# The last batch's second step in one go, its inverse blocks moved behind the first count

## The chip, the cores and the metric

The kernel runs on one core of a Trainium2 chip. The metric is device time in microseconds (us), the median of the runs of a kernel. A profiled run also leaves a trace, whose own time and span stand in the table below. On this core PE (TensorE) does matmuls and transposes, DVE (VectorE), ACT (ScalarE) and POOL (GpSimd) do the elementwise work, and SP (SyncE), ACT and POOL issue DMAs.

## The reference

The input `x` has 8 batches of 2496 tokens with 256 columns. Each batch is filtered along its tokens in the frequency domain; then 19968 tokens go to 8 experts.

```python
X = np.fft.rfft(x, axis=1)
Y = X * (filt_r + 1j * filt_i)[None]
x = np.fft.irfft(Y, n=2496, axis=1).reshape(19968, 256)
logits = x @ w_gate                       # 19968 x 8
order = np.argsort(-logits.flatten())     # greedy, best pair first
for idx in order:
    tok, e = idx // 8, idx % 8
    if assigned[tok] >= 0 or counts[e] >= 2496:
        continue
    assigned[tok] = e; counts[e] += 1
for e in range(8):
    out[assigned == e] = np.maximum(x[assigned == e] @ w1[e], 0) @ w2[e]
```

## The kernel before, in words

**The filter.** 2496 is split into 39 by 64, so each transform has two steps of small matmuls. Per batch, `s1` is the first forward step. `s2` is the second: four matmuls with `cW` (L241), two DVE products with the filter (L247 into `P`, L248 into `Q`), and a POOL subtraction and addition (L249, L250), after which `P` holds a block of the spectrum. There are ten such blocks in a batch, and `Q` has one buffer. `tr` turns blocks with four transposes on PE into PSUM (L260, tile `pa`). `split` casts the turned block on ACT to `yh` (L281), and takes the rest `yl` as the turned block minus `yh` (L282), so that a matmul works with two rounded parts. `inv1` is the first inverse step of one of ten blocks `q`: for each of two halves three matmuls (L296: `cEh` by `yh`, `cEh` by `yl`, `cEl` by `yh`), a copy to `zt` (L308) and two DMAs to a buffer `zd` in DRAM (L310).

**The gate on the side.** The logits are linear in the spectrum. The gate is multiplied into the blocks of the spectrum (L269), the result is turned (`trv`, L288), and `v1` (L328), a transpose (L344), `v2` (L354) and `v3` (`lg`, L356) run the same two inverse steps on the 8 columns of the logits. The routing can begin when the logits of all batches are there, before the tokens themselves.

**The second inverse step.** It is cut into 40 units (a batch and a fifth of its columns). A unit is loaded from `zd` (`load_z`, L377), multiplied by `cD` in three parts (two of 512 columns, one of 256: L403), each part is copied to `xo` (L404), and the unit is stored to `xs` in DRAM (L407). Units of the first two batches run in the transform; the other 30, `rest`, run beside the routing. While the transform's buffers still stand, stores go from two `xo` tiles or from parts of an old `Y1` tile; a new pool takes their place in front of unit 15.

**The routing.** `threshold` searches each expert's threshold in 11 rounds. A round builds the comparison `Gm` on DVE (L564, two pieces), counts with 11 matmuls (L572), takes `t`, `D` and `X` from the count on DVE (L580 to L582), spreads it over all partitions with one matmul (L585, called the broadcast product here), and takes the next threshold from it on DVE (L609, L622, L624, L602, L605). The rounds are a chain PE, DVE, PE, DVE. Then places and lists are made (L712 to L772), tokens are gathered from `xs` with indirect DMAs on POOL (L825), turned (L839) and put through the experts' two matmuls (L861, L904) to the end of the kernel.

**What sets the order.** `run` puts the transform's steps into a list of events with a slot number (ten slots a batch) and a priority, and emits them in order of slot. A scheduler then places each engine's instructions by its own estimate of the timeline, except where `manual_schedule` asks for an engine's order of emission; before, that holds for PE from the first broadcast product on. Beside the rounds, `Pump` takes pieces from the generator `after()`, which yields an estimated cost for each part of a unit and for each of the five `inv1` of the last batch that are left to it. Of the last batch, `q` from 5 are copied by ACT to a buffer `y7` when they are turned (`y7b`), and `split` by ACT and POOL when their `inv1` comes.

Of the kernel before, what the change touches and what calls it, by code (L numbers as in the profile page):

```python
# [15 lines left out]
G = 22  # L16
# [116 lines left out]
class Fft:  # L133


    def __init__(s, tc, i, xs, zd, lg, pp):
        s.tc, s.nc, s.i, s.xs, s.zd, s.lg, s.pp = tc, tc.nc, i, xs, zd, lg, pp
        s.zw = s.zo = s.y7 = s.y9 = None
# [97 lines left out]
    def s2(s, b, g, dh):  # L236

        nc = s.nc
        p = s.ps.tile([128, 4, 128], F32, name="p2", tag="b", bufs=2)
        for k in range(4):  # L240
            nc.tensor.matmul(p[:, k], s.Y1[b][:, 4*g+k, dh*128:dh*128+128], s.cW[:, 4*g+k], start=True, stop=True)  # L241
        P = s.yt[b, g, dh] = s.wp.tile([128, 4, 128], F32, name="P", bufs=NP)
# [9 lines left out]
    def tr(s, b, q):  # L252

        nc = s.nc
        g, k = q // 2, 2 * (q % 2)
        yt = [s.yt[b, g, dh] for dh in range(2)]
        p = s.ps.tile([128, 2, D], F32, name="pa", tag="c", bufs=4)
        for h in range(2):
            for dh in range(2):
                nc.tensor.transpose(p[:, h, 128*dh:128*dh+128], yt[dh][:, k+h], s.id)  # L260
        if b == B - 1 and q > 4:
            nc.scalar.copy(s.y7b(q), p)
        else:
            s.split(b, q, p, nc.vector)
        if k:
            p = s.ps.tile([128, 128], F32, name="pv", tag="c", bufs=4)
            for dh in range(2):
                for k in range(4):
                    nc.tensor.matmul(p[32*k:32*k+32], s.gate[:, dh], yt[dh][:, k], start=dh == 0, stop=dh == 1, skip_group_check=True)  # L269
            s.vs[b, g] = s.wp.tile([128, 128], F32, name="vs", bufs=1)  # L270
            nc.scalar.copy(s.vs[b, g], p)

    def y7b(s, q):
        if q == 9 and s.y9 is None:
            s.y9 = s.wp.tile([128, 4, 128], F32, name="P", bufs=NP).rearrange("p k d -> p (k d)")
        y = s.y7[:, 80+512*q:592+512*q] if q < 9 else s.y9
        return y.rearrange("p (k d) -> p k d", d=D)

# [18 lines left out]

    def inv1(s, b, q):
# [5 lines left out]
        p = s.ps.tile([128, 2, D], F32, name="pa", tag="c", bufs=4)  # L304
# [11 lines left out]
    def v1(s, g, b0, b1):  # L316

        nc = s.nc
        if s.y7 is None:
            s.y7 = s.wp.tile([128, K1 * D], F32, name="Y1", tag="Y1", bufs=2)  # L320
            nc.gpsimd.memset(s.y7[:72, :2640].rearrange("p (a n) -> p a n", n=3*G)[:, :, N2:], 0.0)
        c = 8 * (b1 - b0)
        r = slice(64, 64 + c) if b0 else slice(0, c)
        p = s.pt([128, 4, 128], not b0)
        for k in range(4):
            (h, l), (Eh, El) = ([t[:, 4*g+k] for t in ts] for ts in ((s.Vh, s.Vl), s.cE))
            for m, (v, w) in enumerate(((h, Eh), (h, El), (l, Eh))):
                nc.tensor.matmul(p[:c, k], v[:, 8*b0:8*b1], w, start=m == 0, stop=m == 2)  # L328
        z = s.y7[r, :2640].rearrange("p (r k n) -> p k r n", r=2, k=K1)[:, 4*g:4*g+4, :, :N2]
        nc.scalar.copy(z, p[:c].rearrange("p k (r n) -> p k r n", r=2))  # L330

    def v2(s, b0, b1):
# [3 lines left out]
        s.U = s.zp.tile([120, G, c], F32, name="xo", tag="xo", bufs=2)  # L336
        n = 8 if c > 8 else G
        for g0 in range(0, G, n):
# [8 lines left out]
    def v3(s, b0, b1):  # L347

        nc, c = s.nc, 8 * (b1 - b0)
        n = 8 if c > 8 else G  # L350
        for g0 in range(0, G, n):
            g1 = min(g0 + n, G)
            p = s.pt([128, g1 - g0, c], not b0)
            s.lastv = nc.tensor.matmul(p[:120], s.cD, s.U[:, g0:g1], start=True, stop=True).ins  # L354
            with s.tc.issue_after(s.lastq):
                nc.vector.tensor_copy(s.lg[:, b0:b1, g0:g1], p[:117].rearrange("p g (b e) -> p b g e", e=8))  # L356

    def more_z(s, units):
# [3 lines left out]
        y = s.wp.tile([128, 4, 5, D], F32, name="Y1", tag="Y1", bufs=2)  # L362
        s.xos = [y[:120, k] for k in range(4)]
        zs = [f[:120, k] for k in range(4)] + [w[:120, k] for k in range(2)]
# [45 lines left out]
    def run(s, cp, wp, xp, ps, freed, prep, rest):  # L410
# [13 lines left out]
        for b in range(B):  # L424
# [34 lines left out]
        at(10*B - 0.8, 9, s.more_z, rest[3+NZ:9+NZ])  # L459
        at(10*B + 2.9, 3.61, s.more_z2, rest[9+NZ:3+NZ+MZ])  # L460
        at(10*B + 2.9, 3.6, s.v2, B - 1, B)
        at(10*B + 2.9, 3.62, s.v3, B - 1, B)
        at(10*B + 2.9, 3.64, prep, S - G, S)
        for q in (2, 3, 4):
            at(10*B + 2.9, 3.7 + 0.01 * q, s.inv1, B - 1, q)
        for e in sorted(ev, key=lambda e: e[:3]):
            e[3](*e[4])

# [6 lines left out]
class Route:  # L475
# [75 lines left out]
    def counts(s, nj, thr, made=False):  # L551
# [374 lines left out]
def emit(tc, i, out):  # L926
    nc = tc.nc
    with ExitStack() as st:
# [18 lines left out]
        def freed():  # L947
# [187 lines left out]
```

## Time and profile before

| | us |
|---|---|
| runs of the kernel before | 1430.25, 1433.83, 1435.20; median 1433.83 |
| profiled run, its own time | 1429.82 |
| its span | 1428.0 |
| PE busy | 1380.0 (97%) |
| DVE, ACT, POOL busy | 899.9, 681.3, 487.5 |
| mean granted clock of PE | 0.99 |

The page divides the span into 40 slices of 35.7 us. PE is at 9 tenths or more in all but three: the first, the one from 321 to 357 (8) and the one from 393 to 428 (6), in which the last unit ends and the first gathered tokens arrive, and in which the granted clock is below 9 tenths too:

```profile
PE   8999999998969999999999999999999999999998
PEclk9999999999989999999999999999999999999999
DMA  9676675658881022102212212112111321111100
```

Busy shares are of all time, at whatever clock was granted. "Idle before, releaser" in a row is the engine's idle time ahead of an instruction and what ended it.

### The profile page before, as it was taken

What the parts mean: (1) busy time and instruction counts of PE and PEld (TensorE: products, weight loads), DVE (VectorE), ACT (ScalarE), POOL (GpSimd) and SP (SyncE); (2) the same over time, 40 slices, a digit from 0 to 9 for tenths busy, and PEclk for the clock granted to TensorE, in tenths of its full rate; (3) what the DMA queues carried; (4) which work ended last, traced back from release to release, by engine and by line L of the source; (5) the groups of instructions that cost most, each with busy time, mean ns of one, the idle gap of its engine ahead of it and who ended that gap; (6) DMA issues with size and microseconds to landing.
All of it is one profiled execution on the core that took longest, in us unless ns stands there. A gap on an engine that the chain in (4) does not pass through costs nothing. (4 is left out here: it accounts for less than half of the span.)

```text
span 1428.0 us, 27263 instructions
## 1 busy us (share of the span) xinstructions
PE 1380.0 (97%) x10338; PEld 1210.5 (85%) x10338; DVE 899.9 (63%) x2568; ACT 681.3 (48%) x1658; POOL 487.5 (34%) x538
## 2 busy tenths in 40 slices
PE   8999999998969999999999999999999999999998
PEld 8898898885437898888888888889898899899988
DVE  6677676776547769668667875876867635423231
ACT  7766766644464346226335533533623635423231
POOL 3433433431024126323422632433424333323212
PEclk9999999999989999999999999999999999999999
DMA  9676675658881022102212212112111321111100
GB/s 358 225 223 174 217 217 140 148 130 233 321 314 61 29 82 72 41 23 96 63 36 80 68 43 78 56 43 90 58 34 51 124 71 51 43 45 51 40 19 29
DMA packets 58124, 152.59 MB, mean 107 GB/s; under 512 B 10889, under 2 KB 32137, under 8 KB 54409
## 3 DMA queue, kind: packets, MB, share of 16 engines
q1 hardware_dynamic: 29200, 68.79, 15.9%
q0 software_dynamic: 18416, 60.37, 12.9%
q10 hardware_dynamic: 10377, 21.68, 4.6%
q8 instruction: 82, 1.34, 0.4%
q14 instruction: 49, 0.40, 0.1%
HBM read 87.16 MB, written 63.70 MB: 106 GB/s over the span
## 5 line engine op out<-in xcount | busy, mean ns | idle before, releaser
L904 PE MATMUL py<-w1h,hl 128*128 128x256 f32 x2496 | 485.7, 287 | 1.0 <-DVE hl L872 0.7
L904 PEld LDWEIGHTS py<-w1h,hl 128*128 128x128 f32 x2496 | 403.0, 191 | 7.3 <-issue 3.2
L904 PE MATMUL py<-w1l,hl 128*128 128x256 f32 (+1 forms) x1280 | 359.5, 283 | 0.0
L915 POOL DMA_INDIRECT out<-y,oid x160 | 169.1, 1057 | 506.7 <-ACT y L914 456.5
L867 ACT ACTIVATE hl<-pz 128x512 fp32r<-128x512 f32 (+1 forms) x320 | 187.4, 588 | 226.7 <-PE pz L861 203.1
L861 PE MATMUL pz<-xo,w0h 128*128 128x512 f32 (+1 forms) x640 | 264.3, 413 | 3.0 <-DVE hl L869 1.5
L869 DVE SCALAR_TENSOR_TENSOR hl<-pz,hl 128x512 fp32r<-128x512 f32 x256 | 175.4, 688 | 144.8 <-ACT hl L867 143.4
L861 PE MATMUL pz<-z,w0h 128*128 128x512 f32 (+1 forms) x640 | 248.7, 389 | 0.0
L861 PE MATMUL pz<-xo,w0l 128*128 128x512 f32 (+1 forms) x640 | 248.6, 388 | 0.0
L904 PEld LDWEIGHTS py<-w1l,hl 128*128 128x128 f32 (+1 forms) x1280 | 241.8, 189 | 1.9
L825 POOL DMA_INDIRECT xg<-xs,xid x160 | 170.4, 1065 | 129.8 <-issue 54.2
L914 ACT COPY y<-py 128x256 f32<-128x256 f32 x152 | 56.6, 372 | 305.8 <-PE py L904 262.6
L861 PEld LDWEIGHTS pz<-xo,w0l 128*128 128x128 f32 x640 | 120.8, 189 | 24.1
L861 PEld LDWEIGHTS pz<-xo,w0h 128*128 128x128 f32 x640 | 121.7, 190 | 21.7 <-DVE hl L869 2.3
L861 PEld LDWEIGHTS pz<-z,w0h 128*128 128x128 f32 x640 | 121.7, 190 | 15.7 <-DVE z L843 0.6
L229 ACT COPY Y<-p 64x240 f32<-64x240 f32 (+1 forms) x302 | 115.3, 382 | 23.4 <-PE p L223 16.9
L249 POOL TENSOR_TENSOR P<-P 128x256 f32<-128x256 f32 x80 | 58.9, 737 | 169.4 <-DVE P L247 169.2
L564 DVE TENSOR_TENSOR Gm<-M,thr 117x1232 bf16<-117x1232 f32 (+2 forms) x80 | 104.4, 1315 | 0.2
L223 PE MATMUL p<-cS,xr 117*128 117x120 f32 x688 | 94.0, 276 | 5.9 <-ACT Y L229 2.8
L223 PEld LDWEIGHTS p<-cS,xr 117*128 117x128 f32 x688 | 85.4, 192 | 10.2 <-ACT Y L229 7.5
L241 PE MATMUL p<-cW,Y 128*128 128x128 f32 x640 | 89.7, 277 | 0.7 <-DVE Q L248 0.7
L241 PEld LDWEIGHTS p<-cW,Y 128*128 128x128 f32 x640 | 80.5, 191 | 6.2 <-issue 3.9
(220 smaller groups left out, 2003.5 us busy)
## 6 DMA issues: line engine op xcount, KB each, us to landing
z<-zd SPq DMA_DIRECT2D x26, 600.0 KB, 7.2
zd<-zt SPq DMA_DIRECT2D x120, 128.0 KB, 2.5
xs<-xo ACTq DMA_DIRECT2D x18, 600.0 KB, 6.5
xr<-x SPq DMA_DIRECT2D x6, 1536.0 KB, 10.7
xr<-x SPq DMA_DIRECT2D x6, 1216.0 KB, 9.2
zd<-zt ACTq DMA_DIRECT2D x40, 128.0 KB, 2.8
xs<-xo SPq DMA_DIRECT2D x8, 600.0 KB, 6.4
xr<-x SPq DMA_DIRECT2D x8, 512.0 KB, 6.3
```

Of the source, the lines that this page charges most:

```text
L223: s.lastmm = nc.tensor.matmul(p[:, q-q0, :120], xv[:, q-24*h], s.cS1, start=True, stop=True).ins
L229: c = (nc.vector.tensor_copy if (t == 5 if b else cp) else nc.scalar.copy)(dst, src)
L241: nc.tensor.matmul(p[:, k], s.Y1[b][:, 4*g+k, dh*128:dh*128+128], s.cW[:, 4*g+k], start=True, stop=True)
L249: nc.gpsimd.tensor_tensor(P[:, :, :64], P[:, :, :64], P[:, :, 64:], op=OP.subtract)
L564: nc.vector.tensor_tensor(Gm[:, s0:s1, :m], s.M[:, s0:s1].unsqueeze(2).to_broadcast([117, s1 - s0, m]), thr[:117].unsqueeze(1).to_broadcas ...
L825: s.lastg = s.nc.gpsimd.indirect_dma_start(out=xg[:n], out_offset=None, in_=s.xs, in_offset=bass.IndirectOffsetOnAxis(ap=ids[0][:n, t:t+1] ...
L861: nc.tensor.matmul(p[:, :n], w[:, sl], x[:, k, :n], start=m == 0, stop=m == 5)
L867: s.lasta = nc.scalar.activation(h[:, :n], p[:, :n], AF.Relu).ins
L869: s.R.low = nc.vector.scalar_tensor_tensor(l[:, :n], p[:, :n], 0.0, h[:, :n].bitcast(F32), op0=OP.max, op1=OP.subtract).ins
L904: nc.tensor.matmul(p[:a.stop-a.start], hs[g][f][:, a], b[:, 256*f:256*f+256], start=m == 0, stop=m == 8 * len(terms) - 1, skip_group_check ...
L914: s.lasta = nc.scalar.copy(y, p).ins
L915: st = nc.gpsimd.indirect_dma_start(out=out_rows, out_offset=bass.IndirectOffsetOnAxis(ap=ids[1][:w, 4*g+t:4*g+t+1], axis=0), in_=y[:w], i ...
```

## The change

- `s2` of the last batch is emitted in slots 70 to 74.5, twice as dense as in other batches. Its ten blocks of spectrum all stay: four in parts of `y7`, five in `P` buffers, one in a `zt` buffer.
- All ten `tr` and `inv1` of the last batch leave the transform and go to `after()`, behind the first count, one pair in front of each part of a unit from the fourth unit (`k > 2`). `y7b`, its ACT copies and POOL's `split` are gone: all `yl` are taken by DVE from PSUM.
- The product with the gate is a function of its own (`gates`). Tables `VA`, `VB` and `LATE` place `v1`, `gates`, `trv` and the last `inv1` of batch 6. The logits come in two parts, batches 0 to 5 and 6 to 7, where they were 0 to 6 and 7. The copy of the first part to `lg` is ACT's.
- `FILL` emits eight parts of units (two units and two thirds) in the transform's last slots, ahead of the first count. The loads `more_z` and `more_z2` come earlier.
- The DMAs to `zd` of the last batch, and those of batch 6 from `q` = 5, are issued by SP, no longer by ACT: 30 of 40.
- PE is in emission order from slot 70 on; `run` is a generator that stops there once.
- In all batches `tr` is at slot `o+q+3.1`, which puts it behind `inv1` of `q-2`, where it was ahead of it.

The number of PE matmuls of each kind is the same but for `v1` to `v3`, where columns move from the first part to the second.

```diff
+LATE = 70.6, 71.6, 73.3, 74.8, 74.9
+VA = 70.2, 70.7, 71.2, 72.3, 72.7
+FILL = (74.96, 1), (75.1, 1), (75.3, 1), (75.45, 1), (75.7, 1), (75.9, 3)
...
+        j = 2*g + dh if b == B - 1 else 4
+        if j < 4:
...
+            P = s.y7[:, 2640+512*j:3152+512*j].rearrange("p (k d) -> p k d", k=4)
+        elif j < 9:
+            P = s.wp.tile([128, 4, 128], F32, name="P", bufs=NP)
+        else:
+            P = s.wp.tile([128, 2, D], F32, name="zt", bufs=ZB).rearrange("p h (k d) -> p (h k) d", k=2)
+        s.yt[b, g, dh] = P
...
-        if b == B - 1 and q > 4:
-            nc.scalar.copy(s.y7b(q), p)
-        else:
-            s.split(b, q, p, nc.vector)
+        with s.tc.issue_after(s.lastq) if b == B - 1 else nullcontext():
+            s.split(b, q, p, nc.vector)
+        if k and b < B - 1:
+            s.gates(b, g)
...
-        if (b, q) not in s.yd:
-            s.split(b, q, s.y7b(q), nc.gpsimd)
...
-            (nc.scalar if b >= B - 2 else nc.sync).dma_start(s.zd[b].rearrange("a n c -> n a c")[:N2, 20*r+2*q:20*r+2*q+2], zt[64*r:64*r+64])
+            (nc.scalar if b == B - 2 and q < 5 else nc.sync).dma_start(s.zd[b].rearrange("a n c -> n a c")[:N2, 20*r+2*q:20*r+2*q+2], zt[64*r:64*r+64])
...
-                    at(o + 2*g + dh, 1, s.s2, b, g, dh)
-                at(o + 2*g + 4.5, 3.5, s.trv, b, g)
-            for q in range(10):
-                at(o + q + 3, 3, s.tr, b, q)
-                if b < B - 1 or q < 2:
-                    at(o + q + I1, 4, s.inv1, b, q)
+                    at(o + (2*g + dh) / (1 if b < B - 1 else 2), 1, s.s2, b, g, dh)
+                if b < B - 1:
+                    at(o + 2*g + 4.5 if (b, g) != (B - 2, 4) else o + 12.65, 3.5, s.trv, b, g)
+            for q in range(10 if b < B - 1 else 0):
+                at(o + q + 3.1, 3, s.tr, b, q)
+                at(o + q + I1, 4, s.inv1, b, q) if b < B - 2 or q < 5 else at(LATE[q-5], 4, s.inv1, b, q)
...
+        for z, n in FILL:
+            for _ in range(n):
+                at(z, 5, s.fill)
...
-            q = 5
+            q = 0
...
                 for c in f.inv2_parts(*rest[k], f.cps):
-                    if q < 10:
+                    if k > 2 and q < 10:
+                        f.tr(B - 1, q)
+                        yield 0.9
                         f.inv1(B - 1, q)
                         q += 1
                         yield 0.65
...
-        while pump.kind != 'G':
-            pump.step_main()
-        with tc.issue_after(f.lastv):
+        with tc.manual_schedule(engines={mybir.EngineType.PE}):
+            next(run, None)
             while pump.kind != 'X':
                 pump.step_main()
-        with tc.manual_schedule(engines={mybir.EngineType.PE}):
             while (0, 0) not in pump.tags:
```

PE before, behind the first broadcast product (L585): parts of units (L403) and `inv1` (L296) whose blocks were turned in the transform.

```order
L585 MATMUL rt_4504<-X3_0_3785,ones16_3783 128x24
L403 MATMUL pv_4519<-z_3522,cD_70 120x512
L296 MATMUL pa_4527<-yh_4522,cEh_129 128x256
L296 MATMUL pa_4527<-yl_4523,cEh_129 128x256
L296 MATMUL pa_4527<-yh_4522,cEl_130 128x256
...
L403 MATMUL pv_4537<-z_3522,cD_70 120x256
```

PE in the changed kernel, behind the second broadcast product (L603): a part of a unit (L412), the four transposes of block 2 (L274), its `inv1` (L310), the next part.

```order
L603 MATMUL rt_4459<-X7_0_3792,ones16_3789 128x56
L412 MATMUL pv_4473<-z_3842,cD_70 120x256
L274 MATMUL pa_4477<-fid_126,Y1_3733 128x128 x4
L310 MATMUL pa_4487<-yh_4482,cEh_129 128x256
L310 MATMUL pa_4487<-yl_4483,cEh_129 128x256
L310 MATMUL pa_4487<-yh_4482,cEl_130 128x256
...
L412 MATMUL pv_4500<-z_3844,cD_70 120x512
```

The transposes now stand in front of the matmuls that use their turned block, and nothing of PE stands between the two. In the whole of this stretch, nothing stands there for five of the ten blocks (`q` = 2, 4, 5, 6, 9), one broadcast product for two (0, 7), and a count of 11 matmuls for three (1, 3, 8).

DVE before, behind the second broadcast product: the next threshold and the comparison, then the next count.

```order
L609 TENSOR_REDUCE mx_4516<-rt 128x7
L622 SCALAR_TENSOR_TENSOR o_4597<-mx_4516,pw 128x7
L624 TENSOR_REDUCE di<-o_4597 128x1
L602 SCALAR_TENSOR_TENSOR thr<-di,km,ic 128x7
L605 TENSOR_TENSOR km<-km,di 128x1
L564 TENSOR_TENSOR Gm<-M,thr 117x560
L564 TENSOR_TENSOR Gm<-M,thr 117x672
L580 TENSOR_TENSOR t_4647<-rt,row 112x128
```

DVE in the changed kernel at the same place.

```order
L640 SCALAR_TENSOR_TENSOR o2_4462<-mx7_4405,pw_3782 128x7
L642 TENSOR_REDUCE di_4463<-o2_4462 128x1
L620 SCALAR_TENSOR_TENSOR thr_4466<-di_4463,km_4397,ic_3783 128x7
L623 TENSOR_TENSOR km_4468<-km_4397,di_4463 128x1
L582 TENSOR_TENSOR Gm_3797<-M_3826,thr_4466 117x560
L582 TENSOR_TENSOR Gm_3797<-M_3826,thr_4466 117x672
L296 TENSOR_TENSOR yl_4483<-pa_4477,yh_4482 128x512
L598 TENSOR_TENSOR t1_4525<-rt_4513,row_3781 112x128
L296 TENSOR_TENSOR yl_4510<-pa_4504,yh_4509 128x512
```

The subtraction `yl_4483`, which `inv1` of block 2 needs, stands behind both pieces of the comparison; so it is for blocks 4, 6 and 9.

## Rows read from the trace of the kernel before

**Rows 1.** Windows: length, PE, PEld, DVE, ACT, POOL busy (count), granted clock, DMA share, GB/s.
```profile
150.00:200.00 50.00, 50.00 (x460) 44.63 (x459) 35.87 (x65) 33.47 (x84) 20.23 (x28) 1.00 0.67 197
...
310.00:320.00 10.00, 8.56 (x106) 6.46 (x106) 6.85 (x12) 5.17 (x12) 2.31 (x4) 1.00 0.87 210
320.00:331.00 11.00, 9.16 (x77) 8.10 (x77) 7.71 (x15) 2.93 (x7) 0.65 (x1) 0.84 0.81 200
331.00:350.00 19.00, 15.32 (x88) 9.59 (x86) 11.96 (x32) 10.38 (x21) 5.71 (x5) 1.00 0.79 214
350.00:370.00 20.00, 20.00 (x96) 10.97 (x95) 10.96 (x39) 11.47 (x24) 0.00 (x0) 1.00 0.96 367
370.00:390.00 20.00, 17.71 (x74) 9.10 (x73) 11.02 (x36) 9.14 (x19) 0.00 (x0) 0.91 0.84 281
390.00:412.40 22.40, 20.50 (x76) 10.12 (x73) 12.91 (x81) 18.30 (x47) 0.00 (x0) 1.00 0.95 370
```

**Rows 2.** PE's timeline, 311 to 331: start, busy, instruction, [idle before, releaser].
```profile
311.06 1.04 PE L260 MATMUL pa<-fid,P 128*128 128x128 f32 x8
...
326.78 0.94 PE L354 MATMUL pv<-xo,cD 120*120 120x176 f32 x2 [0.43 <-DVE xo L345]
...
327.74 0.41 PE L296 MATMUL pa<-yl,cEh 128*128 128x256 f32 x1
327.95 0.41 PE L296 MATMUL pa<-yh,cEl 128*128 128x256 f32 x1
...
330.74 0.68 PE L572 MATMUL rt<-A,Gm 117*48 117x128 bf16 x9
```

**Rows 3.** PE's timeline, 331 to 423.
```profile
334.82 0.17 PE L585 MATMUL rt<-X,ones 128*128 128x24 f16 x1 [1.22 <-DVE X L582]
...
348.13 3.27 PE L403 MATMUL pv<-z,cD 120*120 120x512 f32 x8 [1.10 <-ACT xo L404]
351.24 0.78 PE L572 MATMUL rt<-A,Gm 117*128 117x128 bf16 x11
351.86 1.93 PE L403 MATMUL pv<-z,cD 120*120 120x512 f32 x4
...
380.30 1.47 PE L403 MATMUL pv<-z,cD 120*120 120x512 f32 x2 [2.22 <-ACT xo L404]
...
422.82 1.67 PE L839 MATMUL ptr<-id,xg 128*128 128x128 f32 x6 [10.44 <-DMA xg<-xs,xid]
```

**Rows 4.** ACT's timeline and its DMA issues (ACTq), 311 to 380.
```profile
311.69 0.59 ACT L281 CAST yh<-pa 128x512 fp32r<-128x512 f32 x1 [2.02 <-PE pa L260]
...
342.81 0.59 ACT L404 COPY xo<-pv 120x512 f32<-120x512 f32 x1 [3.54 <-DVE Gm L564]
...
344.55 3.12 ACTq L310 DMA_DIRECT2D zd<-zt  x3
...
379.67 1.84 ACT L404 COPY xo<-pv 120x512 f32<-120x512 f32 x4 [4.98 <-DMA xs<-Y]
```

**Rows 5.** DVE's timeline, 312 to 344.
```profile
312.31 0.69 DVE L282 TENSOR_TENSOR yl<-pa,yh 128x512 fp32r<-128x512 f32 x1 [2.30 <-ACT yh L281]
...
341.12 0.22 DVE L609 TENSOR_REDUCE mx<-rt 128x7 f32<-128x56 f32 x1 [0.43 <-PE rt L585]
...
342.03 1.51 DVE L564 TENSOR_TENSOR Gm<-M,thr 117x560 bf16<-117x560 f32 x2
```

**Rows 6.** PE's timeline inside an earlier batch.
```profile
289.89 0.28 PE L296 MATMUL pa<-yl,cEh 128*128 128x256 f32 x1
290.01 0.28 PE L296 MATMUL pa<-yh,cEl 128*128 128x256 f32 x1
```

**Rows 7.** Groups of POOL's instructions, 250 to 350.
```profile
L249 POOL TENSOR_TENSOR P<-P 128x256 f32<-128x256 f32 x19 | 14.0, 735 | 30.7 <-DVE P L247 30.7
...
L282 POOL TENSOR_TENSOR yl<-Y,yh 128x512 fp32r<-128x512 f32 x4 | 5.1, 1283 | 16.7 <-ACT yh L281 15.5 <-PE pv L403 1.2
```

More of the change, by code (lines that the diff above doesn't have):

```diff
@@ L25 @@
 ORD, TF = (1, 0, 0, 1), (3, 5)
+LATE = 70.6, 71.6, 73.3, 74.8, 74.9
+VA = 70.2, 70.7, 71.2, 72.3, 72.7
+VB = (71.7, 72.2, 73.2), (72.6, 73.1, 74.2), (73.6, 74.1, 74.7), (74.6, 74.75, 74.85), (75, 75.2, 75.4)
+FILL = (74.96, 1), (75.1, 1), (75.3, 1), (75.45, 1), (75.7, 1), (75.9, 3)
 I1, C0 = 5, -2
@@ L137, in __init__ @@
         s.tc, s.nc, s.i, s.xs, s.zd, s.lg, s.pp = tc, tc.nc, i, xs, zd, lg, pp
-        s.zw = s.zo = s.y7 = s.y9 = None
+        s.zw = s.zo = s.y7 = None
         s.xos = []
@@ L241, in s2 @@
             nc.tensor.matmul(p[:, k], s.Y1[b][:, 4*g+k, dh*128:dh*128+128], s.cW[:, 4*g+k], start=True, stop=True)
-        P = s.yt[b, g, dh] = s.wp.tile([128, 4, 128], F32, name="P", bufs=NP)
+        j = 2*g + dh if b == B - 1 else 4
+        if j < 4:
+            if s.y7 is None:
+                s.y7 = s.wp.tile([128, K1 * D], F32, name="Y1", tag="Y1", bufs=2)
+                nc.gpsimd.memset(s.y7[:80, :2640].rearrange("p (a n) -> p a n", n=3*G)[:, :, N2:], 0.0)
+            P = s.y7[:, 2640+512*j:3152+512*j].rearrange("p (k d) -> p k d", k=4)
[4 more added lines that the diff above has]
+        s.yt[b, g, dh] = P
         Q = s.wp.tile([128, 4, 128], F32, name="Q", bufs=1)
@@ L250, in s2, with tr @@
         nc.gpsimd.tensor_tensor(P[:, :, 64:], Q[:, :, :64], Q[:, :, 64:], op=OP.add)
-    def tr(s, b, q):
+    def tr(s, b, q, tag="c"):
         nc = s.nc
@@ L256, in tr @@
         yt = [s.yt[b, g, dh] for dh in range(2)]
-        p = s.ps.tile([128, 2, D], F32, name="pa", tag="c", bufs=4)
+        p = s.ps.tile([128, 2, D], F32, name="pa", tag=tag, bufs=4 if tag == "c" else 2)
         for h in range(2):
@@ L260, in tr, with gates @@
                 nc.tensor.transpose(p[:, h, 128*dh:128*dh+128], yt[dh][:, k+h], s.id)
-        if b == B - 1 and q > 4:
-            nc.scalar.copy(s.y7b(q), p)
-        else:
-            s.split(b, q, p, nc.vector)
[L265 to L277, printed above, removed]
+        with s.tc.issue_after(s.lastq) if b == B - 1 else nullcontext():
+            s.split(b, q, p, nc.vector)
+        if k and b < B - 1:
+            s.gates(b, g)
+    def gates(s, b, g):
+        nc = s.nc
+        p = s.ps.tile([128, 128], F32, name="pv", tag="c", bufs=4)
+        for dh in range(2):
+            for k in range(4):
+                nc.tensor.matmul(p[32*k:32*k+32], s.gate[:, dh], s.yt[b, g, dh][:, k], start=dh == 0, stop=dh == 1, skip_group_check=True)
+        if b < B - 1:
+            s.vs[b, g] = s.wp.tile([128, 128], F32, name="vs", bufs=1)
+        else:
+            s.vs[b, g] = s.y7[:, 4688+128*(g%3):4816+128*(g%3)]
+        nc.scalar.copy(s.vs[b, g], p)
     def split(s, b, q, v, eng):
@@ L296, in inv, with inv1 @@
             s.nc.tensor.matmul(p, w, v, start=m == 0, stop=m == 2)
-    def inv1(s, b, q):
+    def inv1(s, b, q, tag="c"):
         nc = s.nc
-        if (b, q) not in s.yd:
-            s.split(b, q, s.y7b(q), nc.gpsimd)
         zt = s.wp.tile([128, 2, D], F32, name="zt", bufs=ZB)
-        p = s.ps.tile([128, 2, D], F32, name="pa", tag="c", bufs=4)
+        p = s.ps.tile([128, 2, D], F32, name="pa", tag=tag, bufs=4 if tag == "c" else 2)
         for h in range(2):
@@ L318, in v1 @@
         nc = s.nc
-        if s.y7 is None:
-            s.y7 = s.wp.tile([128, K1 * D], F32, name="Y1", tag="Y1", bufs=2)
-            nc.gpsimd.memset(s.y7[:72, :2640].rearrange("p (a n) -> p a n", n=3*G)[:, :, N2:], 0.0)
         c = 8 * (b1 - b0)
@@ L336, in v2 @@
         s.U = s.zp.tile([120, G, c], F32, name="xo", tag="xo", bufs=2)
-        n = 8 if c > 8 else G
+        n = 8 if c > 16 else G
         for g0 in range(0, G, n):
@@ L349, in v3 @@
         nc, c = s.nc, 8 * (b1 - b0)
-        n = 8 if c > 8 else G
+        n = 8 if c > 16 else G
         for g0 in range(0, G, n):
@@ L354, in v3 @@
             s.lastv = nc.tensor.matmul(p[:120], s.cD, s.U[:, g0:g1], start=True, stop=True).ins
-            with s.tc.issue_after(s.lastq):
-                nc.vector.tensor_copy(s.lg[:, b0:b1, g0:g1], p[:117].rearrange("p g (b e) -> p b g e", e=8))
+            (nc.vector.tensor_copy if b0 else nc.scalar.copy)(s.lg[:, b0:b1, g0:g1], p[:117].rearrange("p g (b e) -> p b g e", e=8))
     def more_z(s, units):
@@ L362, in more_z @@
         y = s.wp.tile([128, 4, 5, D], F32, name="Y1", tag="Y1", bufs=2)
-        s.xos = [y[:120, k] for k in range(4)]
+        s.xos, s.nstore = [y[:120, k] for k in range(4)], 2
+        s.st_x = s.nc.scalar
         zs = [f[:120, k] for k in range(4)] + [w[:120, k] for k in range(2)]
@@ L445, in run @@
         for g in range(5):
-            at(10*B - V1 + g*V1D, 3.8, s.v1, g, 0, B - 1)
-            at(10*B - 5.2 + 2*g, 3.6, s.v1, g, B - 1, B)
-        at(10*B - V2, 3.8, s.v2, 0, B - 1)
+            at(VA[g], 3.8, s.v1, g, 0, B - 2)
+            at(VB[g][0], 3.8, s.gates, B - 1, g)
+            at(VB[g][1], 3.8, s.trv, B - 1, g)
+            at(VB[g][2], 3.8, s.v1, g, B - 2, B)
+        at(73.7, 3.8, s.v2, 0, B - 2)
+        at(74.65, 3.8, s.v3, 0, B - 2)
         def prep0():
             with s.tc.issue_after(s.lastq):
-                prep(0, G * (B - 1))
-        at(10*B - 0.9, 3.7, s.v3, 0, B - 1)
-        at(10*B - VP, 3.8, prep0)
+                prep(0, G * (B - 2))
+        at(74.95, 3.8, prep0)
+        for z, n in FILL:
+            for _ in range(n):
+                at(z, 5, s.fill)
         def act():
@@ L458, in run @@
             at(10*B - 15, 9, s.load_z, *u)
[L459 to L467, printed above, removed]
+        at(74.55, 9, s.more_z, rest[3+NZ:9+NZ])
+        at(75.45, 9, s.more_z2, rest[9+NZ:3+NZ+MZ])
+        at(75.6, 3.6, s.v2, B - 2, B)
+        at(75.8, 3.62, s.v3, B - 2, B)
+        at(75.8, 3.64, prep, S - 2*G, S)
+        ev.sort(key=lambda e: e[:3])
+        for e in ev:
+            if e[0] < 10*B - 10:
+                e[3](*e[4])
+        yield
+        for e in ev:
+            if e[0] >= 10*B - 10:
+                e[3](*e[4])
 def lag(t, factor=1.3):
@@ L571, in counts @@
             w = min(b, S - b*k) * n
-            nc.tensor.matmul(c[:KL, :w], s.Gm[:, K*k:K*k+KL], s.A[:, b*n*k:b*n*k+w], start=k == 0, stop=k == last, skip_group_check=True)
+            s.lastc = nc.tensor.matmul(c[:KL, :w], s.Gm[:, K*k:K*k+KL], s.A[:, b*n*k:b*n*k+w], start=k == 0, stop=k == last, skip_group_check=True).ins
         t1 = s.wp.tile([128, 128], F32, name="t1", bufs=2)[:K, :b*n].rearrange("p (e s) -> p e s", s=b)
@@ L955, in freed @@
             f.nload = 0
-        f.run(fc, fw, fx, ps, freed, R.prep, rest)
-        f.nload = 0
-        f.cps, f.st_x = (nc.scalar.copy, nc.scalar.copy), nc.scalar
         W = None
@@ L989, in emit @@
         units = after()
+        f.fill = lambda: next(units)
+        run = f.run(fc, fw, fx, ps, freed, R.prep, rest)
+        next(run)
         def room():
```

1 line of the change is left out of this document (added).

## The prediction

> **What bounds the kernel now.** I read the page's slices first: PE is near full outside the stretch from the end of the transform to the first gathered tokens, so a change in the order of work can only pay or cost there. Then the table of windows [rows 1] gives that stretch by stage. In 150 to 200 PE is busy for all 50.00 us, and in 350 to 370 for all 20.00. From 310 to 412.4, where the last unit ends, PE loses time in two forms: it stands idle, or works at a lower granted clock. Then PE's timeline [rows 2, 3] tells what ended each wait, and the timelines of ACT and DVE [rows 4, 5] what those engines did meanwhile. After the last unit PE waits 10.44 us for the first gathered tokens [rows 3], and the experts fill the rest. So the first gather stands a fixed way behind the last unit, and whatever PE loses before it moves the end one for one, if the experts' part stays as it is.
>
> The losses of before, stage by stage [rows 1]:
> - A, 310 to 331: idle 10.00 − 8.56 = 1.44 and 11.00 − 9.16 = 1.84; the clock of 0.84 over 11 us costs 1.76. Sum 5.04. In this stage PE waits for small steps of the gate between engines, the last of them before `v3` (0.43 [rows 2]).
> - B, 331 to 350: idle 19.00 − 15.32 = 3.68, of it 1.22 for `X` of the first round and 1.10 for a copy to `xo` [rows 3]. The copies are late because ACT is held by DMA issues to `zd`: three took 3.12 us of its queue, and another copy came after 3.54 us of idle time [rows 4].
> - C, 370 to 390: idle 2.29, and 0.09 of 20 us in clock, 1.80. Sum 4.09. The wait is 2.22 for a copy to `xo` [rows 3], which had itself waited 4.98 us on ACT for the store of the last `Y` tile [rows 4]: the change of pools at unit 15.
> - D, 390 to 412.4: idle 22.40 − 20.50 = 1.90.
>
> Together 14.71 us. PE's matmuls are the same in number after the change (columns of `v1` to `v3` move between two parts, at the same total), so the change is worth 14.71 less what the new order loses.
>
> **The change part by part.**
>
> *The denser `s2` and the earlier first count (A).* Ten `s2` in five slots ask more of POOL and DVE than of PE: POOL takes two instructions of about 0.735 per block [rows 7], 14.7 us for ten, and `Q` has one buffer. Since the gate's steps of two batches and the late `inv1` of batch 6 stand between, I see cover for PE, and emission order puts it where the table says. What is left is the way from the last `v3` to the first count: 330.74 − 326.78 = 3.96 us before [rows 2], in which PE had `inv1` to do at the lower clock. Three of the eight `FILL` parts are put there; two such parts take 1.93 us [rows 3], three 2.9. That leaves 1.06. The lower bound is 0 (everything covered), the upper one 4 (the fill parts wait for loads or for their PSUM buffers). I take 1.1. If the earlier `s2` fell short by more, PE would show idle time that 150 to 200 does not have.
>
> *`tr` behind `inv1` in all batches.* PE has no idle time in 150 to 200 [rows 1], and the shift is of one block against another: 0, with 1 us either way.
>
> *Ten pairs of `tr` and `inv1` behind the count (B).* In before, the turned block was there long before its `inv1`. Now PE does four transposes and comes at once to the matmul with `yl`, unless something stands between. How long that takes is shown by the last turned blocks of before. Eight transposes begin at 311.06 and take 1.04 [rows 2], so four end at about 311.58. ACT's cast begins at 311.69 and takes 0.59 [rows 4]; DVE's subtraction begins at 312.31 and ends at 313.00 [rows 5]. So `yl` is there 1.42 us behind the fourth transpose. One matmul (`cEh` by `yh`) can go in the meantime, and a step from one to the next is 290.01 − 289.89 = 0.12 [rows 6]. That leaves a hole of 1.30. Nothing covers it for five blocks, and only a broadcast product of 0.19 for two, which I count at nothing: 7 × 1.30 = 9.1. For three blocks a count stands between, which takes PE 351.86 − 351.24 = 0.62 [rows 3]: 3 × 0.68 = 2.0. The floor is 11.1. On top of it: for four blocks DVE does the next comparison first. From the broadcast product's result to the comparison's end it takes 342.03 + 1.51 − 341.12 = 2.42 [rows 5]. A part of a unit and four transposes take some 0.5 to 1.0 and 0.52 of this, and the cast with its start 0.7, so `yl` begins up to 0.7 late, 2.8 for four. And in front of the transposes there is always a part of a unit, whose copy of 0.59 may hold the cast up by 0.1 to 0.2 us: up to 1.6 in ten. Bounds 11.1 and 15.5. I take half the first and none of the second, 12.5. POOL, which loses five subtractions of 1.28 [rows 7], was not what PE waited for.
>
> *DMA issues.* Thirty of the forty issues that held ACT go to SP, whose loads for the units come earlier; the waits of B for `xo` go with them, since ten remain, all before the first count. Rows 4 show what an issue costs the engine: a copy stood 3.54 us behind two or three of them. The Trainium skill, in "DMA: Bandwidth & Descriptors", section "Issuing engines are not separate DMA queues", says that DMAs from any engine run on the same 16 engines, and that issuing from several saves only the sequencer's time, "usually small relative to the DMA itself". If that time were small here too, the copies would still be late, and the sum below would be 2 to 3 us higher; the rows speak against it.
>
> *The change of pools (C).* Before, the stores of the units before it lay in a stretch with the DMA share at 0.96 [rows 1], and PE waited 2.22 for one. After, unit 15 comes at its own place between 0 (store landed in time, clock held) and the same 4.1. The loads are earlier and two and two thirds units have been stored before the first count, so I take half, 2.0.
>
> *The end (D).* Same as before, 1.9. Eleven parts of units stand behind the last product of the places (L772), where three did; the units, not the lists, set the end.
>
> Sum after: 1.1 + 12.5 + 2.0 + 1.9 = 17.5, against 14.7: +2.8. On the profiled run, 1429.82 (1.8 outside its span), that is 1432.6; the median of the runs is 4.0 above the profiled run, so the forecast for the median is 1433.83 + 2.8 = 1436.6. The sum's ends: 0 + 11.1 + 0 + 1.9 = 13.0 and 4 + 15.5 + 4.1 + 1.9 = 25.5, with the `tr` shift of 1 either way 12.0 to 26.5: −2.7 to +11.8, or 1431.1 to 1445.6.
>
> **The rivals.**
>
> *Transfers set the pace of the units (faster).* In 350 to 370 and 390 to 412.4 the DMA engines are at 0.96 and 0.95 [rows 1], while they idle before. If the units' end is bound by transfers, PE's holes cost nothing as long as the transfers start earlier, and FILL and the early loads do that. The idle share before 350 is 11 × 0.19 + 19 × 0.21 = 2.1 + 4.0, and half of that in 370 to 390 (20 × 0.16 / 2) is 1.6: 7.7 us earlier, 1426.1. For it: those shares, and the 4.98 us in which ACT waited for a store. Against it: in 350 to 370 PE is full in spite of 0.96, and none of PE's waits in rows 3 is for a load of `z`.
>
> *The clock falls in the holes (slower).* After stage A, with idle time in bits of under 0.7 us and PE at 8.56 of 10, the granted clock was 0.84 in 320 to 331 [rows 1], and a matmul of `inv1` took 0.41, one every 0.21 [rows 2], where it took 0.28, every 0.12, in the batch before [rows 6]; that is the lower of the two levels, 1.2 against 2.4 GHz. The new stretch has ten holes. Its matmuls: 10 × (0.52 + 0.72) for transposes and `inv1`, eleven parts of units at 0.5 to 0.97, about 8, and six counts of 0.62: 24 us, beside 12.5 of holes, a busy share of 0.66, lower than that of 310 to 320. At the lower clock matmuls take 0.21 / 0.12 = 1.75 times as long. Half the stretch at it adds 24 / 2 × 0.75 = 9.0, and the whole is 1445.6. It decides from the first hole at which the clock falls. Against it: in 331 to 350 the busy share was 15.32 of 19 and the clock stayed at 1.00. The Trainium skill names the pattern in "TensorE: Matmul & The Clock Gate", section "A second HAM failure mode: psum-queue depth-cycling": a kernel whose PE idled briefly between groups of matmuls kept moving between the two clocks. By that rule the price is the 9.0 of this rival.
>
> *The holes and what they replace are equal, or the order does not show (no change).* If the holes stay at the floor and A and C vanish, the result lies inside the measurement; so it does if PE is not held up since the parts of units queue ahead. 1433.8.
>
> **How the numbers follow.** Forecast 0.46 (1436.6), transfers 0.24 (1426.1), clock 0.22 (1445.6), nothing 0.08. A measurement of this kernel tells 0.3%, 4.3 us, from no change: faster is below 1429.5, slower above 1438.1. The forecast's own range holds both "same" and "slower": half each, 0.23 and 0.23. The transfers' case is faster (0.24); the clock's is slower (0.22); nothing is same (0.08). So 0.24, 0.31 and 0.45. The range reaches into both rivals: 1425 to 1447. The forecast's own is 1431 to 1446.
>
> **What would show it.** Right: ten waits of PE ahead of matmuls `cEh` by `yl`, most at about 1.3 us, four longer, with DVE's `yl` as releaser; ACT without the long idle times behind `zd` issues; the first count earlier than 330.74 by some 6 us (ten `tr` and five `inv1` leave, 10 × 0.52 + 5 × 0.72 = 8.8, eight parts of units of some 7 come, and A loses 3.9 less); the last unit's end later than 412.4 by 1 to 6. Wrong: PE holes under 1 us (then the floor falls and the change is faster); a last unit that ends earlier than 412.4 with PE waiting for loads or for stores (transfers); a granted clock well under 1.00 behind the first count (clock); a front before the count with idle time of more than 4 us (then A was mis-sized).

## The result and the profile after

The changed kernel takes 1447.42 us (median of 6 runs, 1444.36 to 1449.73) against 1430.20 for the kernel before in the same comparison: a ratio of 1.0116, 95% interval 1.0102 to 1.0130, so 17 us slower. The forecast was slower by 2.8; the range ended at 1447.0, just under the measured time. The profiled run has a span of 1443.7, 15.7 more than before.

The windows of the changed kernel over the same stretch, columns as in [rows 1]:

```profile
300.00:305.00 5.00, 5.00 (x53) 4.62 (x52) 2.98 (x6) 0.28 (x2) 1.59 (x3) 0.98 0.24 52
305.00:310.00 5.00, 5.00 (x40) 3.86 (x37) 2.55 (x5) 1.42 (x4) 2.54 (x4) 0.67 0.20 29
310.00:320.00 10.00, 9.16 (x77) 5.60 (x76) 7.19 (x9) 5.26 (x13) 0.36 (x1) 1.00 0.97 236
320.00:331.00 11.00, 8.63 (x37) 5.62 (x37) 2.86 (x7) 2.84 (x6) 0.00 (x0) 0.69 0.96 294
331.00:350.00 19.00, 13.57 (x90) 9.37 (x88) 11.67 (x38) 7.50 (x15) 0.00 (x0) 1.00 0.88 271
350.00:370.00 20.00, 14.17 (x99) 10.08 (x97) 11.96 (x34) 8.18 (x16) 0.00 (x0) 1.00 0.48 131
370.00:390.00 20.00, 18.22 (x81) 10.03 (x79) 10.88 (x35) 9.55 (x20) 0.00 (x0) 0.91 0.77 224
390.00:410.00 20.00, 16.25 (x67) 8.14 (x65) 12.22 (x61) 12.39 (x26) 0.00 (x0) 1.00 0.87 271
410.00:430.00 20.00, 18.69 (x53) 9.17 (x53) 5.60 (x41) 15.59 (x46) 0.18 (x1) 0.91 0.95 369
```

Counted as in the prediction, PE loses here: 1.65 in clock in 305 to 310; 0.84 + 2.37 idle and 3.41 in clock in 310 to 331; 5.43 and 5.83 idle in 331 to 370; 1.78 idle and 1.8 in clock in 370 to 390; 3.75 idle in 390 to 410; 1.8 in clock behind that, and 0.3 idle up to the last unit's end. That is 29.0 us, against 14.7 before and 17.5 forecast. Two things about this count. Before, 305 to 310 cost nothing:

```profile
305.00:310.00 5.00, 5.00 (x46) 4.01 (x45) 3.68 (x7) 1.91 (x5) 2.07 (x3) 1.00 0.32 75
```

And the 3.41 is an upper count. The clock was low there for 6.8 us, from 321.9 to 328.7. Of these, 0.4 lie in a wait of PE and 2.9 under 22 transposes, which take 2.96 here (322.37, below) and 2.96 too where the clock is at its upper level (the three edits together, below). So nearer 1.7 is lost there, and nearer 27.3 in all.

PE's timeline of the changed kernel:

```profile
322.37 2.96 PE L353 MATMUL pv<-fid,Y 16*120 16x16 f32 x22 [2.94 <-ACT Y L339]
...
330.76 0.63 PE L590 MATMUL rt<-A,Gm 117*48 117x128 bf16 x8
...
342.76 0.39 PE L310 MATMUL pa<-yh,cEh 128*128 128x256 f32 x1 [1.06 <-ACT yh L295]
343.87 0.39 PE L310 MATMUL pa<-yl,cEh 128*128 128x256 f32 x1 [0.72 <-DVE yl L296]
...
372.40 0.38 PE L310 MATMUL pa<-yl,cEh 128*128 128x256 f32 x1 [0.72 <-DVE yl L296]
...
373.10 1.88 PE L412 MATMUL pv<-F,cD 120*120 120x512 f32 x2
...
397.43 1.12 PE L412 MATMUL pv<-z,cD 120*120 120x512 f32 x2 [1.80 <-ACT xo L413]
...
410.26 1.70 PE L412 MATMUL pv<-z,cD 120*120 120x512 f32 x2 [2.21 <-ACT xo L413]
...
421.02 7.92 PE L412 MATMUL pv<-z,cD 120*120 120x256 f32 x22
439.58 1.81 PE L857 MATMUL ptr<-id,xg 128*128 128x128 f32 x6 [10.63 <-DMA xg<-xs,xid]
```

The first count stands where it stood [rows 2], not 6 us earlier. The last unit ends at 428.94, 16.6 later, and the wait for the first gathered tokens is the same as before (10.63 for 10.44 [rows 3]). So nearly the whole loss lies ahead of the experts (16.8 us by the first gathered tokens), as the prediction had it. The ten holes are there: block 2, shown, waits 1.06 for the cast and 0.72 for the subtraction. All PE waits from 332 to 430 by who ended them (us in total, times, longest):

```profile
PE pa L310 <- ACT yh L295: 6.7, 8, 1.1
PE pa L310 <- DVE yl L296: 5.2, 10, 0.7
PE pv L412 <- ACT xo L413: 4.0, 2, 2.2
PE rt L590 <- DVE A L566: 1.0, 1, 1.0
```

The holes are 6.7 + 5.2 = 11.9 us. The last of them, of 1.78 (1.06 and 0.72), is the idle time of 370 to 390, and the clock was at its lower level right behind it, from 373.1 to 376.5. ACT's timeline shows what stood ahead of the cast of block 2: the issue of a unit's store.

```profile
341.30 0.37 ACT L413 COPY Y<-pv 120x256 f32<-120x256 f32 x1
341.70 0.32 ACTq L416 DMA_DIRECT2D xs<-Y  x1
342.12 0.58 ACT L295 CAST yh<-pa 128x512 fp32r<-128x512 f32 x1 [0.45 <-PE pa L274]
```

It also shows what stood ahead of the 22 transposes at 322.37:

```profile
317.36 0.39 ACT L413 COPY Y<-pv 120x256 f32<-120x256 f32 x1
321.32 0.37 ACTq L416 DMA_DIRECT2D xs<-Y  x1
321.74 0.57 ACT L339 COPY Y<-pv 16x512 f32<-16x512 f32 x1 [3.98 <-DMA F<-zd]
```

The unit's last copy is done at 317.75, but its store is issued at 321.32: it waited for a load to `F`. In the instruction order both name the same DMA semaphore (`DMAHW1`): the program has eight of these, taken in turn by the issues of SP and ACT, and a DMA waits for the one that had its semaphore before. Behind the store on ACT stood the copy that the last transposes of the gate need.

### The profile page after: what moved, and what is told of

The parts are those of the page before. It is cut to its first block, busy times and chain, and to the rows that moved or that the text cites. A ratio compares the mean times of both kernels' runs of the same rounds, so it can differ in the third digit from the quotient of the medians.

```text
span 1443.7 us, 27261 instructions
## 1 busy us (share of the span) xinstructions
PE 1385.6 (96%) x10338; PEld 1211.7 (84%) x10338; DVE 894.8 (62%) x2569; ACT 681.2 (47%) x1657; POOL 480.1 (33%) x533
## 5 line engine op out<-in xcount | busy, mean ns | idle before, releaser
L879 PEld LDWEIGHTS pz<-z,w0h 128*128 128x128 f32 x640 | 121.6, 190 | 15.7 <-DVE z L861 0.6
L263 POOL TENSOR_TENSOR P<-P 128x256 f32<-128x256 f32 x75 | 55.0, 734 | 153.8 <-DVE P L261 153.6
```

The source lines that it names most:

```text
L879: nc.tensor.matmul(p[:, :n], w[:, sl], x[:, k, :n], start=m == 0, stop=m == 5)
```

## The experiments

The runs were compared in three groups, each with the kernel before. It took 1430 to 1431 in the first (the first three edits, and the DMA issues alone) and in the third (the two in which the shift is taken back). In the second (all others) it took 1448.41, where the experts' part is longer in every kernel that was profiled there (PE busy 194 of 200 us from 600 to 800, where it was 197). So ratios are compared, and the time at which PE begins to turn the first gathered tokens: 422.82 before, 439.58 in the changed kernel.

**Transposes one block ahead.** In the changed kernel; the first block is turned ahead of the pairs.

```diff
                     if k > 2 and q < 10:
-                        f.tr(B - 1, q)
-                        yield 0.9
+                        if q < 9:
+                            f.tr(B - 1, q + 1)
+                            yield 0.9
                         f.inv1(B - 1, q)
```

> The changed kernel with the transposes of the last batch one block ahead: those of block q+1 stand in front of the inverse step of block q. Theory of the ledger: PE's ten waits between transposes and inverse step (11.8 us in the changed kernel's trace, 10.8 of them for blocks 1 to 9) move the end one for one, so that 8 to 10.8 us go: 1437 to 1440 us. Rival, transfers pace the units: the share of the DMA engines is 0.95 in the last stage anyway, PE's waits come back there as waits for stores or loads, and the time stays within 3 us of 1447.

Measured: 1434.45, ratio 1.0030 (1.0017 to 1.0042); first gathered tokens at 427.30. Against the changed kernel that is 0.86%, 12.3 us, somewhat over the upper end. PE's waits from 332 to 374:

```profile
PE pa L310 <- ACT zt L320: 1.7, 1, 1.7
PE rt L590 <- DVE Gm L582: 1.6, 5, 0.5
PE rt L590 <- DVE A L566: 1.1, 1, 1.1
PE rt L603 <- DVE X L600: 1.0, 3, 0.7
PE pa L310 <- DVE yl L296: 0.2, 1, 0.2
```

```profile
331.00:350.00 19.00, 15.78 (x116) 11.61 (x116) 15.38 (x44) 9.61 (x19) 0.00 (x0) 1.00 0.83 245
350.00:370.00 20.00, 17.52 (x111) 11.86 (x110) 14.25 (x43) 10.87 (x21) 0.00 (x0) 1.00 0.81 235
370.00:390.00 20.00, 18.39 (x94) 10.11 (x92) 11.14 (x39) 9.95 (x21) 0.00 (x0) 1.00 0.89 279
```

The holes are gone but for 0.2. The rounds, closer together now, wait 2.6 for `Gm` and `X`, and one `zt` buffer 1.7; this one is a wait for a transfer, since ACT's copy there had waited 2.10 for a store to `zd`. So not all of the 12.3 us are holes: 5.6 are idle time in 331 to 370 (11.26 less 5.70), 2 more are idle time behind that, and behind the count the clock falls once (0.91 in 390 to 410) where it fell twice, 1.8 less. Some 3 us are in none of these rows. That transfers pace the units is refuted: without holes the same units run in less time, at a DMA share of 0.81 where it was 0.48.

**The first early store on SP.** ACT is made the engine of the stores not in `more_z` but behind the first unit.

```diff
-        s.st_x = s.nc.scalar
...
+        def act_x():
+            s.st_x = s.nc.scalar
+        at(75.35, 0, act_x)
```

> The changed kernel with the first early store of a unit issued by SP, where ACT issued it and was held for 3.98 us until an earlier load had landed. Theory of the ledger: PE's wait of 2.94 us ahead of the second set of 22 transposes goes, and with it the low clock behind it as far as the wait causes it: 3 us less if the clock stays low there, up to 6.4 less if it doesn't (1441 to 1444.5 us). Rival: the loads behind the store on SP are late by the same 4 us and the units wait for them later, 1447 us within 1.5.

Measured: 1444.21, ratio 1.0087 (1.0060 to 1.0114), 3 to 4 us less; the interval overlaps that of the changed kernel, but the trace agrees, with the first gathered tokens at 436.61, 3.0 earlier. The second set of transposes and the clock around it:

```profile
319.47 2.96 PE L353 MATMUL pv<-fid,Y 16*120 16x16 f32 x22
...
320.00:331.00 11.00, 9.86 (x45) 6.15 (x45) 4.81 (x12) 2.57 (x6) 0.00 (x0) 0.84 0.97 284
```

The wait of 2.94 is gone, the transposes begin 2.9 earlier, the first count 3.15 earlier (327.61). The store still went out late, at 321.62 on SP, but nothing that PE needs stood behind it. Half of the low clock went too (0.84 for 0.69), but that gave nothing: the half that went lay under the transposes, and from their start to the first count it is 8.14 us where it was 8.39. Nor is it shown to come from the edit, since with the transposes one block ahead, where PE still waited 2.66 there, it was 0.84 too.

**The first 22 transposes in pieces** of 8, 8 and 6.

```diff
-        at(73.7, 3.8, s.v2, 0, B - 2)
+        for part, z in enumerate((73.4, 73.7, 74.05)):
+            at(z, 3.8, s.v2, 0, B - 2, part)
```

> The changed kernel with the first set of 22 transposes of the gate (48 rows, in one piece of 2.98 us, behind which the clock was at its lower level from 304.8 to 310.5 though PE was never idle) cut into pieces of 8, 8 and 6 with other work between. Theory: the long piece of narrow work lets the clock fall; cut up, the clock stays at 1.00 and 1.7 us go (1445.7 us). Rival: the narrow matmuls of v1 around it do it, or something else: the clock falls all the same, no change.

Measured: 1444.64, ratio 1.0100 (1.0082 to 1.0117); the interval overlaps that of the changed kernel. In the changed kernel the clock was at its lower level from 304.8 to 308.3 (not to 310.5, as I had written); here it stayed up:

```profile
305.00:310.00 5.00, 5.00 (x52) 3.59 (x52) 2.44 (x5) 2.17 (x6) 2.91 (x4) 1.00 0.38 89
```

So the loss there goes, and the first gathered tokens come at 438.15, 1.4 earlier; but the reason is not settled by this, see below.

**The DMA issues alone, in the kernel before.**

```diff
-            (nc.scalar if b >= B - 2 else nc.sync).dma_start(s.zd[b]
+            (nc.scalar if b == B - 2 and q < 5 else nc.sync).dma_start(s.zd[b]
```

> The kernel before with one part of the change alone: 30 of the 40 DMA issues to zd go from ACT to SP. Theory of the prediction: ACT's copies come on time in 331 to 350, PE's idle time there falls from 3.68 to about 1.5: 2 us less. Rival: SP's loads of units queue behind these issues, which wait for their data and for an earlier DMA each, and the units wait for loads: no gain, or 2 to 4 us more.

Measured: 1431.92, ratio 1.0011 (0.9996 to 1.0026): no gain. Stage B is better and the next is worse (compare [rows 1]):

```profile
331.00:350.00 19.00, 17.18 (x98) 11.24 (x98) 11.55 (x32) 10.83 (x22) 5.17 (x5) 0.96 0.81 214
350.00:370.00 20.00, 17.48 (x86) 9.27 (x83) 10.08 (x33) 9.27 (x20) 0.00 (x0) 1.00 0.95 345
```

Idle time fell from 3.68 to 1.82 and rose from 0 to 2.52. The 2.52 is one PE wait for ACT's copy to a `Y` tile; ACT itself sat for 4.70 us behind a load. The gain is given back one stage later.

**The three edits together.** The diffs of the first three.

> The three edits together on the changed kernel: transposes one block ahead, the first early store on SP, the first 22 transposes in pieces. If the three terms add up as measured alone (13.0, 3.2 and 2.8 us): 1447.4 - 19.0 = 1428.4, which leaves the rest of the change worth 2 us against the kernel before. Rival: what is won ahead of the first count is paid back behind it, since the rounds' chain or the transfers then wait: 1431 to 1434.

Measured: ratio 1.0012 (0.9998 to 1.0025); first gathered tokens at 423.58, first count at 326.42. That is 1.04% under the changed kernel, 14.9 us, where the three alone make 1.3%. PE's waits behind the first count:

```profile
PE pv L412 <- ACT xo L413: 4.4, 3, 2.5
PE rt L594 <- DVE Gm L586: 2.4, 7, 0.5
PE rt L594 <- DVE A L570: 1.1, 1, 1.1
PE rt L607 <- DVE X L604: 1.1, 3, 0.7
```

Undoing three things takes back nearly the whole of the change's loss. The sum of the three is not met, but it misses by less than their intervals leave open. Against the kernel with the transposes one block ahead alone, the first count comes 4.8 us earlier and the first gathered tokens 3.7; so about 1 us is paid back behind the count, where the waits of the rounds are 4.6 (3.7 there). The second set of transposes takes as long at a clock of 1.00 as it did at the lower level:

```profile
319.74 2.96 PE L354 MATMUL pv<-fid,Y 16*120 16x16 f32 x22
```

**The second set in pieces as well.** `FILL` has nine parts, some of them between the pieces.

```diff
-        at(75.6, 3.6, s.v2, B - 2, B)
+        for part, z in enumerate((75.6, 75.7, 75.8)):
+            at(z, 3.6, s.v2, B - 2, B, part)
```

> As the three edits together, and the second set of 22 transposes (16 rows) in pieces as well, with parts of units between, nine of them ahead of the first count. Theory: narrow work in one piece lets the clock fall, in 320 to 331 too (0.84 with the store on SP), so up to 1.8 us more go: 1426.6. Rival: the pieces put the last logits, and with them the first count, later by the parts between, and the clock falls for another reason: the same as the three edits, or 1 us more.

Measured: ratio 1.0006 (0.9989 to 1.0023), the same within the interval. The clock fell all the same, lower than in the kernel where this set is in one piece (first row: this kernel; second row: the three edits together):

```profile
320.00:331.00 11.00, 10.56 (x41) 6.16 (x41) 3.87 (x10) 2.74 (x7) 0.00 (x0) 0.69 0.97 318
```

```profile
320.00:331.00 11.00, 9.86 (x57) 6.82 (x56) 5.24 (x13) 3.89 (x9) 0.00 (x0) 1.00 0.97 285
```

**The shift of the transposes alone, in the kernel before.** `o + q + 3` becomes `o + q + 3.1`.

> The kernel before with one part of the change alone: the transposes of a block behind the inverse step of two blocks earlier, in all batches. The prediction's 0 with 1 either way: 1429 to 1431. Rival: the idle time of PE in 40 to 200, which is 3.9 us in the changed kernel and 1.7 before, comes from this: 1432.4.

Measured: ratio 1.0022 (1.0006 to 1.0038), some 3 us slower, as the rival had it. PE idles 3.06 of 60 us in 40 to 100 (1.74 before) and 0.88 in 100 to 200 (0 before).

**The changed kernel without the early parts.** `FILL = ()`.

> The changed kernel without the eight parts of units ahead of the first count: they stand behind it. Theory of the ledger: PE's work is the same; the store that held ACT is not there, which gives 3 us, but the steps from the last logits to the first count, which three parts covered, stand open for about 2.6 us: 1447 within 1.5. Rival: the early parts are worth their time, since the stores of units set the pace: 4 to 6 us slower, 1452.

Measured: ratio 1.0165 (1.0142 to 1.0189), 0.49% or 7 us slower than the changed kernel: the ledger missed, and the early parts are worth their time. The first count came at 321.44, but the steps ahead of it stood open, and the clock was at its lower level for most of the stage:

```profile
320.00:331.00 11.00, 8.14 (x23) 3.97 (x24) 5.44 (x19) 1.55 (x3) 0.00 (x0) 0.56 0.69 185
```

That parts made later cost time because stores pace the units was not shown: PE's longest waits here are 2.9 for `A` inside the first count and 2.8 for a copy to `xo`, beside the ten holes.

**The shift taken back in the changed kernel.** `o + q + 3.1` becomes `o + q + 3`.

> The changed kernel with the transposes of a block ahead of the inverse step of two blocks earlier again, as in the kernel before. Theory: the shift costs in the changed kernel what it cost alone in the kernel before, 0.22%: the ratio to before falls from 1.0116 to 1.0094. Rival: from the last batch on, where the order is fixed, the front waits for other things, and the shift is hidden: 1.0116.

Measured: ratio 1.0119 (1.0100 to 1.0139): no difference is seen, though the two intervals leave room for some 3 us either way. In the profiled run the gain is lost again: PE idles 1.72 us in 40 to 200, where it idled 3.93 in the changed kernel, but then 2.30 in 250 to 280, where it idled 0, and the clock is 0.84 in 280 to 300, where it was 1.00. The first count comes 1.2 later (331.98).

**The three edits and the shift taken back.** The diffs above.

> The three edits together (transposes one block ahead in the last batch, the first early store on SP, the first 22 transposes in pieces), and the shift of the transposes in the other batches taken back. The three edits gave a ratio of 1.0012 to the kernel before; if the shift costs 0.22% here too, 0.999, a little faster than before. Rival: 1.0012, the shift costs nothing once the rest is mended.

Measured: 1431.67, ratio 1.0001 (0.9988 to 1.0014): as fast as the kernel before, not faster; against the three edits alone the intervals overlap. No version beat the kernel before.

## Why the prediction was right or wrong

- *The bound.* Right. What PE loses between the end of the transform and the last unit moved the end nearly one for one: 14.3 us by the two ledgers (12.6 with 1.7 for the 3.41), 16.6 by the last unit's end. Of the rest, 1.5 us is idle time ahead of 300, 2.2 more in 40 to 200 (3.93 for 1.74), from the shift of `tr` as the experiment on it alone shows, less 0.7 won in 250 to 300. What is left, 1 to 2.5, is in no window's row.
- *The ten holes.* Right in place; right in size partly by luck. Forecast 12.5, 11.9 waited, and 12.3 us gone from the kernel when the transposes stood one block ahead (not all of it holes, as told above). The time was forecast as one wait for `yl`; PE shows two, for the cast and then for the subtraction. Two errors in the terms cancel in part. A block with nothing on top waited 1.04 to 1.10, not 1.30. The comparison on DVE cost the four blocks behind it (2, 4, 6, 9) 0.3 to 0.4 each in the subtraction, 1.4 in all, as forecast. But 2, 6 and 9 waited another 0.34 each for the cast, behind the issue of a unit's store on ACT (341.70), for which the sum has no term. So 4 waited 1.34, and 2, 6 and 9 1.78.
- *The earlier first count (A).* Wrong, and the largest miss: 1.1 forecast, bounds 0 and 4; 8.3 measured (3.21 idle, 3.41 and 1.65 in clock), 6.6 with 1.7 for the 3.41. The step that failed is "What is left is the way from the last `v3` to the first count". That way was covered: PE has no idle time from 327.11 to 330.76. The wait came ahead of it, 2.94 in front of the second set of transposes. I had counted the fill parts' matmuls as cover and not their stores: the first store, on ACT, waited for another engine's load and held the gate's copy for 3.98. The edit that moves only this store gave 3 to 4 us. The other part is clock, which the bound of 4 left out altogether, though [rows 1] shows it in the same stage before (1.76).
- *The DMA issues.* Right for B, wrong for the total. In the changed kernel no wait in 331 to 370 is for a copy to `xo`; but alone, in the kernel before, the gain in B (1.86 less idle) was lost in the next stage. The section "Issuing engines are not separate DMA queues" of the Trainium skill's "DMA: Bandwidth & Descriptors" fits the outcome better than my weighing of it: moving the issues bought only the sequencer's time, and no total (ratio 1.0011).
- *The change of pools and the end (C and D).* In 370 to 430 the ledger has 9.4 (5.83 idle, 1.8 in clock in 370 to 390 and as much in 410 to 430), and 3.9 was forecast; but 1.78 of the idle time is the tenth hole, counted among the holes already, and the clock of 370 to 390 was low right behind it. The change of pools itself cost 1.80 where 2.0 was forecast, but by luck: the earlier loads and stores, my reason for taking half, shortened PE's wait only from 2.22 [rows 3] to 1.80 (397.43), and the rest is that the clock held behind it. The end was right in its wait and wrong in the clock: 2.21 at 410.26, for 1.90 before, and then 1.8 in clock, for which D has no term (1.70 for two matmuls that took 1.02 elsewhere). That wait is not one for a store: ACT was busy with eight activations of the routing, and the copies stood behind them, as in the kernel before (1.89 at 401.83).

```profile
406.13 3.61 ACT L750 ACTIVATE lg<-lg,pen 117x176 f32<-117x176 f32 x7
```

- *`tr` behind `inv1`.* Wrong for the kernel before (3 us, not within 1): [rows 1] was read for 150 to 200 alone, and the idle time came in 40 to 100 (3.06 us for 1.74) and 100 to 200 (0.88 for 0). In the changed kernel no difference was seen.
- *The rivals.* Transfers: refuted by the DMA share of 0.48 in 350 to 370 and by the first experiment. The clock: its time, 1445.6, was nearest, but by luck. It had half of the stretch at the lower level, at 9.0 us; the changed kernel has one fall there, behind the tenth hole, at 1.8, and was at 1.00 through the others, at a busy share of 0.71. The mechanism is there in that small size. The four other versions that keep the ten holes have a fall behind the last one too, and three of them another, within 0.3 us of the hole of 1.78 of block 2, as in the kernel with the first set in pieces:

```profile
331.00:350.00 19.00, 14.92 (x82) 10.00 (x81) 10.81 (x35) 7.36 (x14) 0.00 (x0) 0.91 0.79 243
```

  Of the four versions without the holes, three have no fall between the first count and 390. The clock was low also where PE was busy all the time (305 to 310) and around the waits of 2.94 and 2.21. The rule of the Trainium skill's "TensorE: Matmul & The Clock Gate", section "A second HAM failure mode: psum-queue depth-cycling", is borne out in part: the clock did fall behind one of the ten idle bits, and stayed up behind the rest. Clock losses over the stretch were about 8.7 against 3.6 before (7.0 with 1.7 for the 3.41), 3 to 5 us of the result.
- *Open.* What lets the clock fall around the gate's transposes. The first set uncut was followed by a low clock in three kernels and not in two (without the early parts, and with the shift taken back); cut, it was followed by none in four. Around the second set the clock was low in all versions with the set uncut but one (the three edits), and in the only version with it cut; in the changed kernel it fell 0.4 us ahead of the set, in PE's wait. Narrow work in one piece may be a part of it; alone it does not decide. Why the early parts are worth 7 us, beyond 2.9 of wait and the lower clock ahead of the count, was not told apart either.

## What to carry to other kernels

A step that goes through three engines in a row (turn, cast, subtract) cost PE 0.5 to 1.8 us a block here, and 0.2 in all once the producer stood one block ahead of the consumer in the same order. Count such a chain as so many holes, with what stands in front of each link on its engine. Work used as cover must be counted with its stores: ask what a DMA issue waits for, data and semaphore, and what stands behind it on the issuing engine. And a bound for a stage that has shown a low clock must hold the clock too, counted over the matmuls that take longer at the lower level: 22 narrow transposes took 2.96 us at either.

## What was not expected of the hardware

PE was busy for 5.00 of 5.00 us in 300 to 305 and again in 305 to 310, and its granted clock in the second was 0.67. PE's timeline of the changed kernel, the same matmuls of 16 columns ahead of the fall and behind it:

```profile
297.79 0.23 PE L337 MATMUL pv<-cEl,Vh 128*16 128x128 f32 x1
...
300.77 2.98 PE L353 MATMUL pv<-fid,Y 48*120 48x48 f32 x22
...
304.85 0.30 PE L337 MATMUL pv<-cEl,Vh 128*16 128x128 f32 x1
304.94 0.31 PE L337 MATMUL pv<-cEh,Vl 128*16 128x128 f32 x1
```

They come every 0.06 at the upper level (297.85 the next) and every 0.1 at the lower one, with no idle time of PE between. In 331 to 370, with 5.43 of 19 and 5.83 of 20 us idle in the holes, the clock was 1.00; it fell behind the last hole.
